# Sixteen Strassen blocks in the first matrix of a fused attention and two-matrix kernel, with copied C11 starts and accumulating DMAs

## The chip, the core and the metric

The kernel runs on one core of one Trainium2 chip. Its time is what the device takes for one execution, in microseconds (us). TensorE (PE) multiplies matrices and writes PSUM (8 banks of 128 x 512 f32); VectorE (DVE) and ScalarE (ACT) read PSUM and work on SBUF; GpSimd (POOL) and SyncE (SP) mostly issue DMAs here. Each engine runs its own instructions in order.

## What is computed

Attention with 4 batches, 8 heads, 768 positions and 64 channels, over the last 96 positions and 8 global ones, with a linear bias by distance. Its output, 3072 tokens of 512, goes through two matrices:

```python
scores = scale * q @ k^T + bias          # kept where local (0 <= i-j < 96) or global (j < 8)
x = softmax(scores) @ v                  # 3072 x 512
h = x @ w_in                             # 512 -> 2048
g = h - tanh(h)
out = g @ w_out                          # 2048 -> 512
```

## The kernel before

The 3072 tokens are 24 units of 128 queries. A unit u goes through words (steps) whose order on all five engines is one long string, ORDER, read from left to right and issued as it stands; a second string, HOMES, gives each tile's buffer or PSUM bank. A word is a step, a unit or group, and a part; "/a", "/d", "/p" or "/s" after it puts it on ACT, DVE, POOL or SP. The words that matter here:

- lq, lk, lv: loads of q, k and v by POOL (line 342); T.u: q and k transposed, by TensorE for the first seven units and from u = 7 by SP's DMA transposes (L377); V.u, K.u: copies of the 8 global rows.
- S.u: scores (PE, L396); E.u: exponential (ACT, L403); M.u: mask (DVE); AV.u: P·V (PE, L427); R, N: division by the sums (DVE, L433, L444); X or Xe: x transposed, by PE or by SP's DMA (L466).
- First matrix: units form groups of 1, 2 or 4. Plainly, m1.g.f are the matmuls of one block (L477), th.g.f the tanh (ACT, L576), g.g.f the subtraction to g (DVE, L590).
- A Strassen block (g, j) of the first matrix, four units by four slices of 128 columns: seven products d1 to d7 (in_product, L536) of 4 matmuls 128 x 256, in place of 8 halves; e0, e1, e2 copy partial results out of PSUM, q11, q21, q22 add (L547, L550), and tanh and subtraction take two slices at once (L562, L568). x and w_in sums (y and v) feed them.
- Second matrix, in pairs of units, all Strassen: n1 to n4 sum g (L630), p1 to p7 are the products (L645, 8 matmuls 128 x 256), a0 to a2 copy partial results (line 274 on ACT, 276 on DVE), c11 to c22 form results (L659), st stores (L662). w1 to w4 are the sums of w_out.

POOL's queue holds all loads and half the stores in order; SP's queue the DMA transposes and the other stores. A DMA on either that must wait (for a buffer, a landed load) holds all that is behind it.

Of the kernel before, what the change touches and what calls it, by code (L numbers as in the profile page):

```python
# [7 lines left out]
FP32 = mybir.dt.float32  # L8
BF16 = mybir.dt.bfloat16
# [8 lines left out]
lq.1 lk.1 zero rel ones.0 zero:7 dist lq.2 lq.0 lk.0 zero:7 zero:7 table lq.3 turn zero:7 first zero:7 lk.3 ident slopes  # L18
zero:7 zero:7 lk.2 ones.1 B.0 lv.1 cq.1/a ck.1/d bm.1 lv.0 T.1.1 em.1 lv.2 T.1.0 Te.1.1/d B.1 cq.0/a lv.3 Te.1.0/d
ck.0/a T.0.0 S.1 in.0 Te.0.0/a T.3.0 B.2 E.1.0 in.1 Te.3.0/d T.0.1 Te.0.1/d in.3 T.2.1 T.3.1 Te.2.1/a T.2.0 Te.3.1/d S.0  # L20
lq.4 Te.2.0/a AV.1 E.0.0 S.2 R.1 N.1/d in.2 B.3 E.2.0 lk.4 AV.0 S.3 R.0 N.0/d X.1 in.4 E.3.0 AV.2 Xe.1/d X.0 in.5 R.2
N.2/d bm.2 Xe.0/a AV.3 m1.1.0 lk.5 em.2 R.3 N.3/d X.2 m1.0.0 th.1.0 Xe.2/d X.3 lq.5 th.0.0 g.1.0 m1.0.2 Xe.3/a g.0.0
m1.1.2 th.0.2 m1.2.2 th.1.2 g.0.2 g.1.2 lv.4 m1.2.6 th.2.2 lk.6 g.2.2 T.4.0 th.2.6 m1.2.0 Te.4.0/a m1.1.4 lq.6 th.2.0
m1.0.4 lv.5 th.1.4 g.1.4 T.4.1 m1.2.4 Te.4.1/a g.2.0 th.0.4 S.4 th.2.4 g.0.4 out.1 m1.1.8 K.4/a E.4.0 g.2.6 m1.2.8
th.1.8 M.4.0 E.4.1 m1.0.8 g.1.8 th.2.8 out.0 M.4.1 m1.0.12 th.0.8 g.2.4 out.2 T.5.1 g.2.8 T.5.0 Te.5.1/a m1.1.12 out.3
Te.5.0/d th.0.12 g.0.8 S.5 lk.7 th.1.12 g.0.12 AV.4 E.5.0 g.1.12 lq.7 m1.2.12 n1.0/d E.5.1 lk.10 m1.2.10 M.5.0 lq.10
V.4/a R.4 m1.2.14 M.5.1 th.2.10 K.5/d N.4/d AV.5 th.2.14 T.6.1 X.4 R.5 Te.6.1/a T.6.0 N.5/d lq.9 Xe.4/a Te.6.0/d X.5 S.6
Xe.5/d g.2.14 m1.3.2 E.6.1 n3.0/d m1.3.10 g.2.10 lq.8 th.2.12 w1.1 th.3.2 p1.0 E.6.0 w1.0 m1.3.12 g.2.12 a0.0/a g.3.2
m1.3.4 lk.8 th.3.12 n2.0/d K.6/a th.3.10 m1.3.0 w2.0 m1.3.8 w4.0 w2.1 lk.9 p2.0 M.6.0 p6.0 lv.7 g.3.12 w3.1 T.7 m1.3.6
lv.6 a1.0/a c11.0 th.3.0 w3.0 p5.0 g.3.10 p7.0 a2.0/a n1.2/d th.3.4 g.3.0 p1.2 th.3.6 n2.2/d p2.2 a0.2/a w4.1 th.3.8  # L30
c22.0 p6.2 V.5/a n4.2/d T.8 p4.0 n3.2/d a1.2/a g.3.8 T.9 p5.2 g.3.6 p7.2 c21.0 a2.2/a T.10 g.3.4 st.1.0/p p3.2 M.6.1
lk.11 c11.2 S.7 c12.2/a c22.2 lv.11 n4.0/d AV.6 E.7.1 p4.2 lk.12 R.6 N.6/d E.7.0 m1.3.14 lv.9 K.7/d V.6/d M.7.1 X.6
lk.16 th.3.14 p3.0 M.7.0 Xe.6/a c21.2 lq.11 AV.7 g.3.14 c12.0/a lk.13 R.7 S.8 N.7/d lq.12 n1.4/d X.7 E.8.1 p1.4 Xe.7/d
lv.10 n2.4/d m1.4.8 K.9/a E.8.0 v1.1 st.2.0/p n3.4/d m1.4.10 th.4.8 a0.4/d lv.8 g.4.8 p6.4 th.4.10 v2.1 E.9.0 lq.13
m1.4.14 g.4.10 M.8 a1.4/a S.9 th.4.14 T.11 p5.4 g.4.14 E.9.1 V.7/d p2.4 a2.4/d E.10.0 M.9 T.12 m1.4.2 E.10.1 n4.4/d
m1.4.6 K.10/a st.0.0/s M.10 AV.9 th.4.6 m1.4.0 th.4.2 g.4.6 m1.4.4 R.9 T.13 N.9/d p7.4 g.4.2 th.4.4 Xe.9 th.4.0 g.4.4
AV.8 V.9/a p3.4 c11.4 c22.4 R.8 m1.4.12 N.8/d c12.4/a st.4.0/p g.4.0 p4.4 Xe.8 th.4.12 lq.15 v3.1 S.10 c21.4 lk.15
g.4.12 p1.6 E.12.0 lv.13 n1.6/d p2.6 n2.6/d a0.6/a lq.14 E.11.1 K.12/d AV.10 lk.14 p6.6 E.11.0 R.10 c11.6 V.10/d lq.16
m1.5.10 N.10/d a1.6/a K.11/a n4.6/d lv.12 S.11 th.5.10 n3.6/d T.15 p5.6 g.5.10 E.12.1 v1.3 m1.5.8 E.13.1 M.12 m1.5.14
a2.6/a th.5.8 T.14 M.11 m1.5.12 E.13.0 m1.5.6 v3.3 th.5.12 Xe.10 v4.1 th.5.14 g.5.12 p3.6 th.5.6 g.5.8 T.16 AV.11 g.5.14  # L40
m1.5.2 g.5.6 m1.5.0 V.11/d th.5.2 R.11 N.11/d c12.6/a p7.6 th.5.0 st.6.0/p g.5.2 Xe.11 lk.17 AV.12 g.5.0 m1.5.4 c22.6
# [24 lines left out]
q22.9.2 d2.9.3 n2.18/d p1.18 q21.9.1 g.9.2 d4.9.2 a0.18/a d5.9.3 n4.16/d d7.9.3 e2.9.3/a q11.9.3 p7.16 th.9.6 q22.9.3
d3.9.3 c11.16 a2.16/a p6.18 n3.18/d q21.9.2 m1.9.3 g.9.6 p3.16 th.9.3 c22.16 a1.18/a d4.9.3 th.9.12 g.9.3 p5.18 q21.9.3
th.9.10 g.9.12 p4.16 a2.18/a p2.18 g.9.10 th.9.14 p7.18 c12.16/a n4.18/d st.16.0/p p1.20 c22.18 g.9.14 p3.18 a0.20/a
p4.18 n1.20/d n2.20/d p2.20 n3.20/d p6.20 n1.22/d c21.16 p7.20 n4.20/d a1.20/a st.17.0/p p5.20 n3.22/d c21.18 p2.22
c11.18 a2.20/a st.19.0/s n2.22/d c12.18/a p1.22 st.18.0/s c22.20 c11.20 p4.20 a0.22/a c11.22 p6.22 n4.22/d st.22.0/s  # L70
c21.20 p7.22 a1.22/a st.21.0/p p5.22 p3.20 a2.22/a c22.22 p3.22.0 c12.20/a p4.22 st.20.0/s c12.22.0/d st.22.256/s
p3.22.1 c21.22 c12.22.1/d st.23.0/s st.22.384/s
"""
HOMES = """
v.0:1 tr.0.1:6 tr.0.0:6 kq.0:2 qk.0:6 v.1:0 tr.1.1:6 tr.1.0:7 kq.1:0 qk.1:5 v.2:2 tr.2.1:7 tr.2.0:5 kq.2:1 qk.2:8 v.3:3
tr.3.1:4 tr.3.0:7 kq.3:3 qk.3:7 v.4:4 tr.4.1:3 tr.4.0:1 kq.4:4 qk.4:9 v.5:5 tr.5.1:4 tr.5.0:5 kq.5:0 qk.5:18 v.6:6
tr.6.1:7 tr.6.0:1 kq.6:1 qk.6:4 v.7:4 kq.7:0 qk.7:16 v.8:8 kq.8:1 qk.8:3 v.9:5 kq.9:17 qk.9:2 v.10:6 kq.10:19 qk.10:10
# [44 lines left out]
def kernel(  # L122
# [27 lines left out]
    WJ = 4  # L150
# [692 lines left out]
```

## Time and profile before

| | |
|---|---|
| time, median of 3 runs | 202.04 us (201.58 to 202.12) |
| span of the profiled execution, first to last instruction | 199.8 us |
| what lies between the two | 2.2 us |
| PE, DVE, ACT, POOL busy | 97%, 89%, 68%, 38% |
| matmuls | 2219 |
| clock granted to TensorE | 1.000 |
| moved by DMA | 27.36 MB |

The profiled execution's own time is given as its span; the median of the runs is the time that the kernel is measured by. Busy time adds overlapping matmuls and is not TensorE at its peak. In a row of a group the columns are busy time, mean ns of one, and idle time of the engine before it with what ended that; in a row of the chain or the timeline they are start, length and what ran.

### The profile page before, as it was taken

The numbers are of one execution on the slowest core, as the hardware profiler recorded it, in microseconds if no ns is written. First come the engines' busy times: TensorE is split into PE (matmuls) and PEld (weight loads), VectorE is DVE, ScalarE is ACT, GpSimd is POOL, SyncE is SP. The second block draws the span as 40 slices with busy tenths as digits, with TensorE's granted clock in tenths as the row PEclk, the third lists the DMA queues.
The fourth block names the chain that finished last, engine by engine and source line by source line (L and its number), as shares of the span: only waits on it lengthen the run. The fifth ranks groups of instructions, "written<-read, shape, count | busy, mean of one in ns | idle before, by whom it ended". The sixth has DMA issues, their size and how long they took to land.

```text
span 199.8 us, 5524 instructions
## 1 busy us (share of the span) xinstructions
PE 193.1 (97%) x2219; PEld 157.8 (79%) x2219; DVE 178.6 (89%) x348; ACT 135.1 (68%) x234; POOL 75.3 (38%) x97
## 2 busy tenths in 40 slices
PE   8799999999999999999999999999999999999992
PEld 2469998888888988988898655688898687888892
DVE  6487599999999999999999898999999999999942
ACT  3698898726569559758947789578778777464220
POOL 8987576350694057069207904702000100001110
PEclk9999999999999999999999999999999999999999
DMA  5999999999999999989996998994733101001233
GB/s 148 211 180 185 198 163 207 201 156 141 193 167 196 178 153 135 133 188 171 137 158 146 140 173 192 154 155 85 55 108 121 66 0 54 3 0 52 107 132 131
DMA packets 103545, 27.36 MB, mean 137 GB/s; under 512 B 93920, under 2 KB 101472, under 8 KB 103520
## 3 DMA queue, kind: packets, MB, share of 16 engines
q0 software_dynamic: 74048, 16.78, 89.5%
q1 hardware_dynamic: 28928, 9.70, 27.6%
q10 hardware_dynamic: 544, 0.52, 1.0%
q8 instruction: 17, 0.28, 0.5%
q14 instruction: 8, 0.07, 0.1%
HBM read 27.26 MB, written 6.29 MB: 168 GB/s over the span
## 4 chain that ended last, share of the span: by engine, by line
PE 85%; DVE 7%; DMA 3%; ACT 2%; issue 1%; ACTq 0%; DVEq 0%
PE ps L645 36%; PE ps L477 27%; PE ps L536 9%; PE ps L396 5%; PE ps L427 5%; DMA f<-in_q_dram 3%; DVE gall L590 2%; DVE x L444 2%; DVE mem L407 1%; PE ps L455 1%; ACT mem L403 1%; PE ps L320 1%; ACT mem L274 1%; PE ps L365 1%; ACT th L576 1%
## 5 line engine op out<-in xcount | busy, mean ns | idle before, releaser
L477 PE MATMUL ps<-xT,w_in_bf 128*128 128x256 bf16 (+2 forms) x544 | 69.0, 279 | 0.0
L477 PEld LDWEIGHTS <-w_in_bf 128*128 128x128 bf16 x544 | 47.2, 98 | 12.4
L576 ACT ACTIVATE th<-ps 128x512 f32<-128x512 f32 (+1 forms) x74 | 41.8, 591 | 18.7 <-PE ps L477 13.6
L590 DVE TENSOR_TENSOR gall<-ps,th 128x512 bf16<-128x512 f32 (+1 forms) x74 | 47.4, 668 | 6.0 <-ACT th L576 5.6
L645 PEld LDWEIGHTS <-gall 128*128 128x128 bf16 x488 | 46.4, 98 | 7.0
L662 POOL DMA_DIRECT2D out_dram<-ot x14 | 8.1, 580 | 102.5 <-ACT ot L274 52.4
L403 ACT ACTIVATE mem<-ps 128x1024 bf16<-128x1024 f32 x44 | 43.3, 1024 | 4.3 <-PE ps L396 4.2
L645 PE MATMUL ps<-w_out_bf,gall 128*128 128x256 bf16 (+1 forms) x296 | 36.3, 270 | 0.0
L274 ACT COPY sn<-ps 128x256 f32<-128x256 f32 x32 | 12.0, 375 | 20.3 <-PE ps L645 16.3
L645 PE MATMUL ps<-f,ss 128*128 128x256 bf16 x192 | 24.9, 273 | 0.0
L645 PE MATMUL ps<-wc,gall 128*128 128x256 bf16 x192 | 24.9, 273 | 0.0
L342 POOL DMA_DIRECT2D vb<-in_v_dram x24 | 21.5, 900 | 2.2 <-issue 1.0
L645 PEld LDWEIGHTS <-ss 128*128 128x128 bf16 x192 | 18.3, 98 | 2.8
L342 POOL DMA_DIRECT2D mem<-in_k_dram x20 | 17.9, 899 | 4.8 <-DMA w_out_bf<-in_moe_w_out_dram 3.1
L342 POOL DMA_DIRECT2D mem<-in_q_dram x20 | 18.1, 904 | 3.8 <-DMA w_out_bf<-in_moe_w_out_dram 3.0
L412 DVE TENSOR_TENSOR mem<-mem,mk 128x2048 bf16<-128x2048 bf16 x16 | 19.2, 1215 | 0.0
L659 DVE TENSOR_TENSOR ot<-ps,sn 128x256 f32<-128x256 f32 x36 | 14.7, 415 | 3.6 <-ACT sn L274 2.5
L444 DVE TENSOR_TENSOR x<-ps,rden 128x512 bf16<-128x512 f32 x23 | 15.8, 687 | 0.5
L274 ACT COPY mem<-ps 128x512 f32<-128x512 f32 (+1 forms) x22 | 12.7, 585 | 5.1 <-PE ps L536 3.9
L427 PEld LDWEIGHTS <-mem 128*128 128x128 bf16 x352 | 13.4, 97 | 2.1 <-ACT mem L403 0.5
L427 PE MATMUL ps<-vb,mem 128*128 128x65 bf16 x352 | 14.7, 193 | 0.0
L396 PE MATMUL ps<-mem 64*128 64x128 bf16 x352 | 13.1, 217 | 0.0
(78 smaller groups left out, 220.7 us busy)
## 6 DMA issues: line engine op xcount, KB each, us to landing
out_dram<-ot POOLq DMA_DIRECT2D x14, 256.0 KB, 2.8
vb<-in_v_dram POOLq DMA_DIRECT2D x24, 128.0 KB, 6.2
mem<-in_q_dram POOLq DMA_DIRECT2D x22, 128.0 KB, 6.3
mem<-in_k_dram POOLq DMA_DIRECT2D x22, 128.0 KB, 6.1
out_dram<-ot SPq DMA_DIRECT2D x9, 256.0 KB, 2.0
w_out_bf<-in_moe_w_out_dram POOLq DMA_DIRECT2D x4, 512.0 KB, 10.7
w_in_bf<-in_moe_w_in_dram POOLq DMA_DIRECT2D x4, 256.0 KB, 7.6
w_in_bf<-in_moe_w_in_dram POOLq DMA_DIRECT2D x2, 512.0 KB, 11.0
```

Of the source, the lines that this page charges most:

```text
L274: nc.scalar.copy(out=out, in_=in_)
L342: eng(e).dma_start(out=dst, in_=rows_of(src, u).rearrange("h p d -> p h d"))
L396: nc.tensor.matmul(bank(("s", u, o), hh)[:, p * P : (p + 1) * P], buf(("qk", back[u] if o else u))[r, 1, p, :], buf(("qk", u))[r, 0, p, :] ...
L403: nc.scalar.activation(d, banks(("s", u, o), 0, 1), AF.Exp, bias=0.0, scale=scale)
L412: nc.vector.tensor_tensor(out=t, in0=t, in1=mk[:, 1:3], op=ALU.mult)
L427: nc.tensor.matmul(t[:, h // (H // 2), h % (H // 2), :], buf(("p", u, o))[:, slot(h), :], buf(("v", back[u] if o else u))[:, h, 0 : Dh + 1 ...
L444: nc.vector.tensor_tensor(out=buf(("x", u)).rearrange("q (a h) d -> q a h d", a=2), in0=t[:, :, :, 0:Dh], in1=rden.to_broadcast([P, 2, H / ...
L477: nc.tensor.matmul(t[:, (f - f0) * n : (f - f0 + 1) * n], w_in_bf[j][:, c, fo : fo + P], x[:, c, 0:n], start=(c == 0), stop=(c == CD - 1),)
L536: nc.tensor.matmul(t[:, r * 2 * P : (r + 1) * 2 * P], w(r)[:, c], x[:, c], start=first and r + c == 0, stop=c == 1, skip_group_check=not f ...
L576: nc.scalar.activation(h_view(buf(("th", g, f0)), g, m), h_view(bank(("h", g, f0)), g, m), AF.Tanh, bias=0.0, scale=1.0)
L590: nc.vector.tensor_tensor(out=o, in0=v(h), in1=v(th), op=ALU.subtract)
L645: nc.tensor.matmul(bank((holder, a))[:, c0:c1], s(f), t(f)[:, c0:c1], start=first and f == 0, stop=f == HF - 1, skip_group_check=not first,)
```

## The change

Sixteen blocks (groups 5 to 8, all four j) of the first matrix are Strassen blocks, in place of six; units 8 to 11 form one group of four in place of two pairs. In both matrices the first product that starts C11 is copied by ACT from its PSUM bank to C11's bank (a0, e0), and the second product (p2, d2) adds to it there, so that C11 is a plain copy and the additions q11 go. In groups 6 to 8 the z sums are copied by ACT to memory (x21, x22) and added by accumulating DMAs from POOL (q21, q22); nine n3 and five n4 are accumulating DMAs too. Eight of the V copies are made by SP's DMA. The signs of the w_out sums, the layout of g and the columns of a Strassen product in its bank are others, and ORDER and HOMES are new throughout.

```diff
-    NM, NV, NG, NSS, NSN = 23, 12, 5, 5, 4
+    QUADS = 8
+    NM, NV, NG, NSS, NSN, NXT = 20, 12, 5, 3, 4, 3
-    DUNITS = [(8, 1), (8, 2), (8, 3), (9, 1), (9, 2), (9, 3)]
+    DUNITS = [(g, j) for g in range(5, 9) for j in range(4)]
+    ADDED = range(6, 9)
...
-    groups = [[u] for u in range(SINGLE)] + [[u, u + 1] for u in range(SINGLE, 12, 2)] + [[u, u+1, u+2, u+3] for u in range(12, NU, 4)]
+    groups = [[u] for u in range(SINGLE)] + [[u, u + 1] for u in range(SINGLE, QUADS, 2)] + [
+        [u, u + 1, u + 2, u + 3] for u in range(QUADS, NU, 4)]
...
     def a_V(e, u):
-        copy(e, buf(("v", u))[0:G, :, 0:Dh], buf(("v", head[u]))[0:G, :, 0:Dh])
+        o, i = (buf(("v", t))[0:G, :, 0:Dh] for t in (u, head[u]))
+        if e is SP:
+            nc.sync.dma_start(out=o, in_=i)
+        else:
+            copy(e, o, i)
...
     def in_product(g, j, k):
...
-            2: ("q", lambda r: w_in_of(a + r, 2), x_block(g, 2, 1), True),
+            2: ("q", lambda r: w_in_of(a + r, 2), x_block(g, 2, 1), False),
...
-        t = d_bank(g, j, part)
+        t = d_bank(g, j, part).rearrange("q (t r n) -> q t r n", t=2, r=2)
         for r in range(2):
             for c in range(2):
                 nc.tensor.matmul(
-                    t[:, r * 2 * P : (r + 1) * 2 * P], w(r)[:, c], x[:, c], start=first and r + c == 0, stop=c == 1,
+                    t[:, :, r, :], w(r)[:, c], x[:, c], start=first and r + c == 0, stop=c == 1,
...
     def d_add(g, j, k):
-        if k == 0:
-            q = d_bank(g, j, "q")
-            nc.vector.tensor_tensor(out=q, in0=q, in1=d_keep(g, j, 0), op=ALU.add)
-            return
         a = d_keep(g, j, k)
+        if g in ADDED:
+            nc.gpsimd.dma_start(out=a, in_=buf((f"z{k}", g, j)), accum_op=ALU.add)
+            return
         nc.vector.tensor_tensor(out=a, in0=d_bank(g, j, "z"), in1=a, op=ALU.add)
...
     def g_sum(e, a, k):
...
+        if e is POOL:
+            nc.gpsimd.dma_start(out=o, in_=y, accum_op=ALU.add)
+        else:
+            eng(e).tensor_tensor(out=o, in0=x, in1=y, op=ALU.add)
...
     def keep(e, a, k):
-        copy(e, buf(("sn", a, k)), bank(("r", a))[:, 0:DH2])
+        copy(e, buf(("sn", a, k)) if k else bank(("q", a))[:, 0:DH2], bank(("r", a))[:, 0:DH2])
...
     def result(e, a, i, j, c0=0, c1=DH2):
-        if (i, j) == (1, 2):
-            copy(e, o, bank(("r", a))[:, c0:c1])
+        if i == 1:
+            copy(e, o, bank(("qr"[j - 1], a))[:, c0:c1])
             return
-        holder, k = {(1, 1): ("q", 0), (2, 1): ("z", 1), (2, 2): ("z", 2)}[i, j]
-        nc.vector.tensor_tensor(out=o, in0=bank((holder, a))[:, 0:DH2], in1=buf(("sn", a, k)), op=ALU.add)
+        nc.vector.tensor_tensor(out=o, in0=bank(("z", a))[:, 0:DH2], in1=buf(("sn", a, j)), op=ALU.subtract)
...
+            if g in ADDED:
+                op((f"x2{k}", g, j), ACT, lambda e, g=g, j=j, k=k: copy(
+                    e, buf((f"z{k}", g, j)), d_bank(g, j, "z")))
...
 ORDER (two stretches)
-g.2.8 T.5.0 Te.5.1/a m1.1.12 out.3
-Te.5.0/d th.0.12 g.0.8 S.5 lk.7 th.1.12 g.0.12 AV.4 E.5.0 g.1.12 lq.7 m1.2.12 n1.0/d E.5.1 lk.10 m1.2.10 M.5.0 lq.10
+out.3 lk.9 lv.6 lq.8 T.5.0
+g.2.8 Te.5.1/a m1.1.12 th.0.12 lv.20 Te.5.0/d lk.7 lq.7 T.7 lk.8 g.0.8 v1.0 S.5 th.1.12 g.0.12 AV.4 E.5.0 g.1.12
...
 HOMES (the words of units 7 and 8)
-v.7:4 kq.7:0 qk.7:16 v.8:8 kq.8:1 qk.8:3
+kq.7:5 v.7:5 kq.8:10 v.8:4
+qk.7:12 qk.8:5
```

kq is where a unit's q and k are loaded, qk where their transposes go; the number is the buffer of mem.

How the order moves on POOL, behind the last load of w_out. vb6 and vb7 are the v of units 6 and 20, mem the q and k of a unit. Before, the first two rows of mem are k and q of unit 7 (lk.7, lq.7):

```order
31 L348 DMA w_out_bf3_79<-in_moe_w_out_dram 128x4x512
32 L342 DMA mem_81<-in_k_dram 128x8x64
33 L342 DMA mem_81<-in_q_dram 128x8x64
34 L342 DMA mem_81<-in_k_dram 128x8x64
35 L342 DMA mem_81<-in_q_dram 128x8x64 x3
36 L342 DMA mem_81<-in_k_dram 128x8x64 x2
37 L342 DMA vb4_86<-in_v_dram 128x8x64
38 L342 DMA vb6_88<-in_v_dram 128x8x64
39 L662 DMA out_0_dram<-ot1_114 128x512
```

Now they are lk.9, lv.6, lq.8, lv.20, then lk.7 and lq.7, lk.8 and lq.9, and the accumulating n3.0:

```order
31 L356 DMA w_out_bf3_79<-in_moe_w_out_dram 128x4x512
32 L350 DMA mem_81<-in_k_dram 128x8x64
33 L350 DMA vb6_88<-in_v_dram 128x8x64
34 L350 DMA mem_81<-in_q_dram 128x8x64
35 L350 DMA vb7_89<-in_v_dram 128x8x64
36 L350 DMA mem_81<-in_k_dram 128x8x64
37 L350 DMA mem_81<-in_q_dram 128x8x64
38 L350 DMA mem_81<-in_k_dram 128x8x64
39 L350 DMA mem_81<-in_q_dram 128x8x64
40 L651 DMA gall_102<-gall_102 128x1024
```

The loads of unit 7 have moved from the first and second place to the fifth and sixth.

On ACT, before, from the last exponentials (E.23, first row) on; mem<-ps of 512 are e1 and e2 and e0, sn is a0, vb the copies V.21 and V.22:

```order
118 L403 ACTIVATE mem<-ps 128x1024 x2
119 L274 COPY mem<-ps 128x512
120 L274 COPY sn_111<-ps 128x256
121 L274 COPY vb_88<-vb_85 8x8x64
122 L274 COPY mem<-ps 128x512
123 L576 ACTIVATE th<-ps 128x512
124 L274 COPY mem<-ps 128x512 x2
125 L562 ACTIVATE th<-ps 128x1024
126 L274 COPY mem<-ps 128x512
```

Now, with the exponentials of units 20 to 23 (L412) among tanh of two slices (L578), copies x21 and x22 to mem and the copies e0 from bank to bank (ps<-ps 512); the last row of them here is e0.7.0:

```order
134 L578 ACTIVATE th<-ps 128x1024
135 L412 ACTIVATE mem<-ps 128x1024 x3
136 L578 ACTIVATE th<-mem 128x1024
137 L412 ACTIVATE mem<-ps 128x1024 x3
138 L578 ACTIVATE th<-mem 128x1024
139 L282 COPY mem<-ps 128x512 x2
140 L412 ACTIVATE mem<-ps 128x1024
141 L282 COPY ps<-ps 128x512
142 L412 ACTIVATE mem<-ps 128x1024
143 L282 COPY mem<-ps 128x512 x2
144 L282 COPY ps<-ps 128x512
```

The Strassen steps of groups 6 and 7 now stand among the last units' exponentials, where before they came behind them.

More of the change, by code (lines that the diff above doesn't have):

```diff
@@ L68 @@
[L68 to L72, printed above, removed]
+lk.1 lq.1 zero zero:7 zero:7 zero:7 zero:7 zero:7 zero:7 zero:7 rel ones.0 lq.2 dist lk.0 lq.0 lq.3 turn table first
@@ L478, in m1 @@
                     t[:, (f - f0) * n : (f - f0 + 1) * n], w_in_bf[j][:, c, fo : fo + P], x[:, c, 0:n],
-                    start=(c == 0), stop=(c == CD - 1),
+                    start=f == f0 and c == 0, stop=(c == CD - 1),
+                    skip_group_check=f > f0,
                 )
@@ L494, in wsum @@
     def wsum(j, k):
-        return four(("ws", j))[:, k - 1]
+        return ws[:, j, k - 1]
     def xsum(g, k):
@@ L758 @@
         for k in range(3):
-            op((f"e{k}", g, j), None, lambda e, g=g, j=j, k=k: d_copy(e, g, j, k))
-        for w, k in (("q11", 0), ("q21", 1), ("q22", 2)):
-            op((w, g, j), DVE, lambda e, g=g, j=j, k=k: d_add(g, j, k))
+            op((f"e{k}", g, j), None if k else ACT, lambda e, g=g, j=j, k=k: d_copy(e, g, j, k))
+        for w, k in (("q21", 1), ("q22", 2)):
+            op((w, g, j), POOL if g in ADDED else DVE, lambda e, g=g, j=j, k=k: d_add(g, j, k))
+            if g in ADDED:
+                op((f"x2{k}", g, j), ACT, lambda e, g=g, j=j, k=k: copy(
+                    e, buf((f"z{k}", g, j)), d_bank(g, j, "z")))
     for x in range(2):
```

268 lines of the change are left out of this document (142 added, 126 removed).

## The prediction

> **What bounds the kernel now.** I read the page's busy times and slices first, then the chain that ended last, then the timelines of the queues around the places that the change moves.
>
> ```profile
> span 199.8 us, 5524 instructions
> PE 193.1 (97%) x2219; PEld 157.8 (79%) x2219; DVE 178.6 (89%) x348; ACT 135.1 (68%) x234; POOL 75.3 (38%) x97
> PE   8799999999999999999999999999999999999992
> DVE  6487599999999999999999898999999999999942
> PEclk9999999999999999999999999999999999999999
> DMA  5999999999999999989996998994733101001233
> PE 85%; DVE 7%; DMA 3%; ACT 2%; issue 1%; ACTq 0%; DVEq 0%
> ```
>
> TensorE is the bound: busy in every slice, at an even clock, and 85% of the chain. VectorE is close behind (89%), ScalarE has room on average, and the DMA engines are full for the first two thirds. So a matmul that is saved is worth its time only if neither VectorE, ScalarE nor a transfer becomes late in the same stretch. The chain gives the price of each kind of TensorE work, since its rows carry no overlap:
>
> ```profile
> 15.41 0.45 PE ps L477 x8
> 25.79 0.92 ACT mem L403
> 34.92 0.56 PE ps L396 x16
> 43.57 0.87 PE ps L477 x8
> 52.31 0.55 PE ps L396 x16
> 62.61 0.78 PE ps L396 x24
> 66.99 0.48 PE ps L427 x16
> 152.52 0.44 PE ps L536 x4
> 178.65 17.12 PE ps L645 x160
> 195.80 0.42 DVE ot L659
> ```
>
> A block of the first matrix (L477: 8 matmuls 256 wide, or as many columns in other widths) takes 0.87, a Strassen block's one product (L536) 0.44, one of the second matrix's (L645) 17.12/20 = 0.86, scores of one unit (L396) 0.55 or 0.78, P·V (L427) 0.48. I count from the end of S.4, the scores of unit 4, because everything ahead of it is the same work in nearly the same order (16.7 us of TensorE in both):
>
> ```profile
> 23.46 0.62 PE L396 MATMUL ps<-mem 64*128 64x128 bf16 x16
> 24.01 3.73 PE L477 MATMUL ps<-xT,w_in_bf 128*128 128x128 bf16 x56
> 56.71 0.84 PE L396 MATMUL ps<-mem 64*128 64x128 bf16 x24
> ```
>
> From 24.0 to the end of the last product at 195.8 are 171.8 us; the work in it, counted from the program at those prices, is 168.7. So TensorE waits 3.1 us in all: up to the end of S.8 (57.5, where 32.0 us of work make 56.0) 1.5, behind it 1.6. The remaining 4.0 are the last result, the last stores and the end. The profiled 199.8 stand 2.2 under the median of the runs, 202.04; I add every difference to the median.
>
> **TensorE work: -4.4.** Behind S.4 the scores, P·V, transposes and the second matrix's products are the same in number. The first matrix's 64 plain blocks become 24, and its Strassen products 42 become 112: 40 x 0.872 off, 70 x 0.436 on, 34.9 - 30.5 = 4.4 us less. That C11 starts from a copied bank changes no count: p2 and d2 only stop clearing their bank.
>
> **VectorE: -11 of work, nothing by itself.** Rows that price what goes and comes:
>
> ```profile
> L590 DVE TENSOR_TENSOR gall<-ps,th 128x512 bf16<-128x512 f32 x70 | 45.8, 682 | 5.5 <-ACT th L576 5.2
> L659 DVE TENSOR_TENSOR ot<-ps,sn 128x256 f32<-128x256 f32 x36 | 14.7, 415 | 3.6 <-ACT sn L274 2.5 <-PE ps L645 0.8
> L630 DVE TENSOR_TENSOR gall<-gall 128x1024 bf16<-128x1024 bf16 x12 | 8.2, 681 | 0.0
> L568 DVE TENSOR_TENSOR gall<-ps,th 128x1024 bf16<-128x1024 f32 x6 | 7.3, 1219 | 0.0
> L550 DVE TENSOR_TENSOR mem<-ps,mem 128x512 f32<-128x512 f32 x12 | 8.2, 682 | 0.0
> ```
>
> Off: 40 plain subtractions (27.3), 14 g sums (9.5), 12 result additions (5.0), 10 Strassen additions (6.8). On: 20 subtractions over two blocks (24.4), x and w_in sums (some 5) and some 15 copies out of PSUM that the new order gives to it (9). That is 11 less, but VectorE is not what TensorE waits for in most of the program, so it only gives slack. In one stretch it gets tighter: the w_in and w_out sums that stood behind 37 us now stand between M.4.0 and the first products, where VectorE is full already; by the same prices I find 1.8 us more of its work there than of TensorE's. That lies ahead of S.7 and inside the next term.
>
> **Transposes of units 7 and 8: +6.0, the largest term.** Here are the two queues as they ran, POOL with the loads and SP with the transposes of q and k. The three landing lines are those of the loads (L342) from 28 to 46 us, of the transposes (L377) from 38 to 54, and of all 17 transposes; the last two rows are the page's DMA issues:
>
> ```profile
> 27.45 0.74 POOL L348 DMA_DIRECT2D w_out_bf<-in_moe_w_out_dram  x1
> 28.62 0.89 POOL L342 DMA_DIRECT2D mem<-in_k_dram  x1 [0.43 <-PE ps L356]
> 29.50 0.88 POOL L342 DMA_DIRECT2D mem<-in_q_dram  x1
> POOL mem L342 <- DMA w_out_bf<-in_moe_w_out_dram: 6.0, 4, 1.9
> DMA to landing us min/median/max: 6.5/10.7/13.7
> 43.24 1.33 SPq L377 DMA_TRANSPOSE mem<-mem  x1
> 46.73 4.26 SPq L377 DMA_TRANSPOSE mem<-mem  x2
> DMA to landing us min/median/max: 5.0/5.8/8.3
> DMA to landing us min/median/max: 3.1/5.4/8.3
> vb<-in_v_dram POOLq DMA_DIRECT2D x24, 128.0 KB, 6.2
> out_dram<-ot POOLq DMA_DIRECT2D x14, 256.0 KB, 2.8
> ```
>
> The loads of unit 7 are the two rows at 28.62 and 29.50, right behind the last load of w_out. They queue behind it on full DMA engines: the longest landing of this window is 13.7 us, and 29.50 + 13.7 = 43.2 is when T.7 is issued. T.7 has the 8.3 (43.24 + 8.3 = 51.5), and S.7 starts at 52.31 without a wait: before, it was just in time. Now four loads (lk.9, lv.6, lq.8, lv.20) stand ahead of those two. Each is 0.88 of issue, and the queue passes them at about that pace, so lq.7 lands 4 x 0.88 = 3.5 later and T.7 is issued at 46.8. T.8, which was issued at 46.73 beside T.7, now writes where T.7 reads: its queue holds it until T.7 has landed. Behind it on SP wait T.10, V.7 and T.12.
>
> At the median of all, 5.4 for a transpose, T.7 lands at 52.2 and T.8 at 57.6. Between S.4 and S.7 stand 23.0 us of TensorE work (16 blocks of the first matrix, 6 products, 3 P·V, 2 scores, the small transposes), 4 us less than before, since six products moved behind it and a P·V and a block ahead of it; from S.7 to S.8 0.5 + 2.6. So without waits S.8 would start at 24.0 + 23.0 + 3.1 = 50.1, and it waits to 57.6: 7.5 us, the VectorE stretch within them. From this I take off the 1.5 that before loses up to there: **+6.0**. Bounds: with the fastest, 3.1, for both, 46.8 + 6.2 = 53.0, 2.9 of wait, +1.4; with 8.3 and 5.5, 60.6, 10.5 of wait, +9.0.
>
> The Trainium skill (Advanced Engine Details and Errata, "X-Bar Transpose (TRN2)") says that transpose DMAs on this chip are as fast as regular DMAs. Here they are not quicker than the loads, 5.4 against 6.2, but slower than a store of 256 KB, 2.8; at that price T.7 and T.8 would land at 46.8 + 5.6 = 52.4, 2.3 of wait, which would make the term +0.8 and the whole -1.4, rival A's side.
>
> **ScalarE: +2.2 in one stretch.** Prices:
>
> ```profile
> L403 ACT ACTIVATE mem<-ps 128x1024 bf16<-128x1024 f32 x44 | 43.3, 1024 | 4.3 <-PE ps L396 4.2
> L562 ACT ACTIVATE th<-mem 128x1024 f32<-128x1024 f32 x6 | 6.4, 1059 | 1.4 <-DVE mem L550 1.2 <-DVE gall L568 0.2
> L274 ACT COPY mem<-ps 128x512 f32<-128x512 f32 x18 | 10.3, 585 | 4.1 <-PE ps L536 3.9
> L274 ACT COPY sn<-ps 128x256 f32<-128x256 f32 x32 | 12.0, 375 | 20.3 <-PE ps L645 16.3 <-DVE ot L659 3.4 <-DVE mem L509 0.5
> ```
>
> Back to back each takes 0.10 less than its mean (scores' exponential 1.024 in the group, 0.92 in the chain). ScalarE gets about 23 us more to do: 40 tanh of 512 go, 20 of 1024 come, some 29 copies of 512 to memory, and 28 copies from bank to bank, which no row shows. Those I bound by the nearest rows of the same sizes, 0.585 and 0.375 (a copy that stays in PSUM could be a tenth quicker or slower), and take the rows. On average this fits: 172 of 200. It does not fit between e1.6.1 and e0.7.0: two copies at the ends, 8 exponentials, 7 tanh, 12 copies of 512 and one of 256 are 8 x 0.92 + 7 x 0.95 + 14 x 0.48 + 0.27 = 21.0 us, while TensorE has 18.8 us of work between d6.6.1, which frees the first, and d6.7.0, which needs the last: +2.2 at least, if ScalarE is never idle there. Taken 1.0 lower if the copies are quicker, 1.0 higher for one late accumulation.
>
> **Edits at nothing, with their cover.** The 38 accumulating DMAs are not in the trace; issue 0.58 as a store of 256 KB, landing between the store's 2.8 and a load's 6.2. I take 2.8, since most of the 24 for z fall behind 140 us, where the DMA slices empty, and then each lands before the tanh or product that wants it; at 6.2 they cost (rival B). They also queue on POOL in order, and n3.0 and q22.6.2 there hold the loads behind them. The eight V copies by SP cost VectorE and ScalarE nothing; two stand between T.7 and T.10. The end: c21.20 (0.42) and a store of 256 KB (2.0 on SP, 2.8 on POOL) against 0.42, 0.29 and a store of 64 KB (1.8): 0 to +0.8, taken 0. The 1.6 us of TensorE's waits behind S.8 stay.
>
> **Sum:** -4.4 + 6.0 + 2.2 = +3.8, so 199.8 + 3.8 = 203.6 for the span and 202.04 + 3.8 = **205.8** for the time. With the low ends, -4.4 + 1.4 + 1.2 = -1.8: 200.2; with the high ends, -4.4 + 9.0 + 3.2 + 0.8 = +8.6: 210.6.
>
> **Rivals.** *A, the transposes come in time.* If lq.7 lands where the load in its place landed before with less queued behind it, and transposes run at 3.1, S.7 and S.8 wait only for VectorE's stretch, which is about the 1.5 that before lost too: -4.4 + 0.3 + 2.2 = -1.9, 200.1, and 198.1 if ScalarE's stretch finds 2 us elsewhere. For it: POOL's next instruction behind the loads, n3.0, waits for VectorE, and then fewer loads crowd the transposes. Against: 5.0 was the least that any took in that window. It decides when T.8 lands before 57.6 - 3.8 = 53.8, where the sum is 0.
>
> *B, accumulating DMAs gate the tanh.* At a load's 6.2 each accumulation is 3.4 later. th.6.10 and th.6.14 stand in ScalarE's full stretch with about 1.5 of slack, and p3.4 waits for n4.4, which is issued behind some twenty loads: 2 x (3.4 - 1.5) + 1.5 = +5.3 on top, 211. For it: POOL is in order, the last loads stand between the accumulations of group 6, and the DMA slices up to 140 us are full. Against: from there they are at 4 to 7 tenths and below.
>
> *C, the strided output.* The Strassen products now write two runs of 128 per row of the bank instead of one of 256. The nearest row, blocks of the first matrix 128 wide, is hardly dearer per column (8 in 0.45 in the chain's row at 15.41, against half of 0.87), so it is 0 in the sum; twice the time for 448 matmuls would be 448 x 0.109 = +49, 255 us. The Trainium skill (PSUM — Partial Sum Buffer, "Specifications (TRN2)") says that any non-contiguous access pattern slows matmuls significantly, which speaks for C; no run here shows such a pattern.
>
> **How the numbers follow.** The forecast has 0.52, A 0.30, B 0.15, C 0.03. Medians of this kernel differ by some 0.3%, 0.6 us, so faster means below 201.4 and slower above 202.6. A is mostly below: 0.29 in all. Between lies the forecast's low edge, 0.07. Slower gets 0.64. The range takes A's middle and part of B: 199.5 to 210.5.
>
> **What would show it.** Right: S.7 and S.8 start late behind SP's transposes, TensorE idle 4 to 9 us between 45 and 60 us, put down to DMA mem; later a wait of about 2 us for ScalarE's copies or tanh around the stretch of units 20 to 23; L536 matmuls at the same price. Wrong: TensorE dense from 47 to 60 us (A), waits for POOL's DMAs ahead of L578 or behind n4.4 (B), L536 matmuls dearer (C), or a new wait that none of these names.

## The result, and the profile after

The changed kernel takes **296.07 us** (294.67 to 298.54, 3 runs) against 202.04, a ratio of 1.466 [1.4536, 1.4785]. Slower was the likelier side, but 205.8 with a range up to 210.5 missed by 90 us, so the right direction says little for the forecast. The lines of the page that answer to those of before:

```profile
span 292.8 us, 5747 instructions
PE 214.8 (73%) x2275; PEld 173.9 (59%) x2275; DVE 175.9 (60%) x319; ACT 158.2 (54%) x263; POOL 106.2 (36%) x131
PE   8899779645877179828977676676773869877793
DVE  6657899816636068764865157365572467648752
ACT  4977766735448138426754367654770467654410
PEclk9999999968979759986997689777998899999999
DMA  7999999999999963999124249996089556685243
PE 7%; DVE 2%; ACT 0%; issue 0%; DVEq 0%
```

No engine is full: TensorE falls from 97% to 73%, VectorE from 89% to 60%. The matmuls are as many as was counted, 2275: 224 of the plain blocks less and 280 of Strassen products more than 2219. From the fifth slice on (some 29 us) TensorE has gaps, and from the eighth (51 us) it is rarely full, as are the others: they wait for each other. The chain can be followed back only over the last 10% of the span. The granted clock (PEclk), which stood at 9 in every slice before, now dips. Where the waits end, six rows of the view of all waits (us in total, times, longest):

```profile
ACT mem L282 <- PE ps L550: 29.2, 18, 6.9
ACT mem L412 <- PE ps L404: 18.2, 8, 6.2
PE ps L668 <- ACT mem L412: 14.6, 8, 3.0
DVE x L457 <- DMA xT<-x: 10.9, 4, 6.0
PE ps L440 <- ACT mem L412: 5.8, 4, 3.1
PE ps L404 <- DMA mem<-mem: 2.1, 1, 2.1
```

The third row is the odd one. L668 are the second matrix's products and L412 the scores' exponentials: they share no data. The timeline shows one case, in which they share no bank either: S.8 (from there on one S takes the scores of a unit and a half, here unit 8 and half of unit 9), its three exponentials, and p7.0:

```profile
59.31 0.85 PE L404 MATMUL ps<-mem 64*128 64x128 bf16 x24 [2.13 <-DMA mem<-mem]
60.24 2.85 ACT L412 ACTIVATE mem<-ps 128x1024 bf16<-128x1024 f32 x3 [2.65 <-PE ps L404]
63.15 1.23 PE L668 MATMUL ps<-wc,gall 128*128 128x256 bf16 x5 [2.99 <-ACT mem L412]
```

The exponentials end at 60.24 + 2.85 = 63.09, and p7.0 starts 0.06 later after a wait of 2.99. By HOMES p7.0 writes bank 4 (z.0:4) and the last exponential, E.8.1, reads banks 1 and 5 (s.8.1:1,5). Bank 4 is touched by neither half; it lies between them. This is what the experiments went after first: an instruction on two banks is written as one access with a step, `ps[:, x : y + 1 : y - x, :]`, and every two-bank access of before has neighbours, (0,1) to (6,7), while most pairs of after lie apart: 73 of the 124 instructions of ScalarE and VectorE on two banks, against none of 105 before.

### The profile page after: what moved, and what is told of

The parts are those of the page before. It is cut to its first block, busy times and chain, and to the rows that moved or that the text cites. A ratio compares the mean times of both kernels' runs of the same rounds, so it can differ in the third digit from the quotient of the medians.

```text
span 292.8 us, 5747 instructions
## 1 busy us (share of the span) xinstructions
PE 214.8 (73%) x2275; PEld 173.9 (59%) x2275; DVE 175.9 (60%) x319; ACT 158.2 (54%) x263; POOL 106.2 (36%) x131
## 5 line engine op out<-in xcount | busy, mean ns | idle before, releaser
L668 PEld LDWEIGHTS <-gall 128*128 128x128 bf16 x488 | 50.0, 105 | 24.8 <-issue 13.9
L412 ACT ACTIVATE mem<-ps 128x1024 bf16<-128x1024 f32 x44 | 43.3, 1025 | 23.6 <-PE ps L404 18.2
L561 POOL DMA_DIRECT2D mem<-mem x24 | 21.3, 984 | 78.4 <-ACT mem L282 57.1
L282 ACT COPY mem<-ps 128x512 f32<-128x512 f32 (+1 forms) x51 | 29.2, 587 | 32.6 <-PE ps L550 29.2
L550 PE MATMUL ps<-mem,ws 128*128 128x256 bf16 x192 | 30.6, 292 | 21.4 <-ACT mem L282 8.1
L550 PEld LDWEIGHTS <-ws 128*128 128x128 bf16 x256 | 26.1, 103 | 29.2 <-issue 24.7
L668 PE MATMUL ps<-w_out_bf,gall 128*128 128x256 bf16 (+1 forms) x296 | 38.7, 281 | 5.2 <-ACT mem L412 3.4
L668 PE MATMUL ps<-wc,gall 128*128 128x256 bf16 x192 | 29.1, 308 | 9.0 <-ACT mem L412 3.6
L668 PE MATMUL ps<-f,ss 128*128 128x256 bf16 x192 | 27.9, 297 | 7.6 <-ACT mem L412 7.6
L490 PE MATMUL ps<-xT,w_in_bf 128*128 128x256 bf16 (+1 forms) x320 | 31.9, 253 | 1.2 <-DVE gall L608 1.0
L608 DVE TENSOR_TENSOR gall<-ps,th 128x512 bf16<-128x512 f32 (+1 forms) x34 | 21.8, 656 | 14.1 <-ACT th L593 9.0
L584 DVE TENSOR_TENSOR gall<-ps,th 128x1024 bf16<-128x1024 f32 x16 | 19.6, 1223 | 13.0 <-ACT th L578 7.1
L668 PEld LDWEIGHTS <-ss 128*128 128x128 bf16 x192 | 20.1, 105 | 11.6 <-issue 7.7
L593 ACT ACTIVATE th<-ps 128x512 f32<-128x512 f32 (+1 forms) x34 | 18.9, 578 | 10.5 <-PE ps L490 7.5
L578 ACT ACTIVATE th<-ps 128x1024 f32<-128x1024 f32 x16 | 16.4, 1025 | 12.9 <-DVE mem L563 5.0
```

The lines of the kernel that those rows point to most:

```text
L282: nc.scalar.copy(out=out, in_=in_)
L412: nc.scalar.activation(d, banks(("s", u, o), 0, 1), AF.Exp, bias=0.0, scale=scale)
L490: nc.tensor.matmul(t[:, (f - f0) * n : (f - f0 + 1) * n], w_in_bf[j][:, c, fo : fo + P], x[:, c, 0:n], start=f == f0 and c == 0, stop=(c = ...
L550: nc.tensor.matmul(t[:, :, r, :], w(r)[:, c], x[:, c], start=first and r + c == 0, stop=c == 1, skip_group_check=not first or r > 0,)
L561: nc.gpsimd.dma_start(out=a, in_=buf((f"z{k}", g, j)), accum_op=ALU.add)
L578: nc.scalar.activation(d_tanh(g, f), h_of(g, f), AF.Tanh, bias=0.0, scale=1.0)
```

## The experiments

Medians are in us. The kernel before measured 202.04, 201.54, 201.5, 201.78 and 201.71 in the groups of runs; ratios are to it.

**The kernel before with its banks renumbered.** One permutation of bank numbers in HOMES, by which the neighbours (0,1) become 0 and 4, and so on; order, work and data are the same:

```diff
- s.8.0:6,7  s.8.1:2,3  av.8:4,5 ...
+ s.8.0:3,7  s.8.1:1,5  av.8:2,6 ...   # 0,1,2,3,4,5,6,7 -> 0,4,1,5,2,6,3,7 throughout
```

> The kernel before with its eight PSUM banks renumbered (0 1 2 3 4 5 6 7 become 0 4 1 5 2 6 3 7) and nothing else: same order, same work, same buffers. Every access to two banks at once, which was to neighbours, now goes to banks four apart. Theory R (an access to two banks that lie apart is made to wait, and be waited for, as if it covered every bank between them): much slower, 260 us or more, with TensorE waits of 1 to 4 us ended by exponentials and subtractions of other banks. Theory A (the 94 us come from the accumulating DMAs and the queues behind them): 202.0, no change within 0.3%.

Measured: **276.55**, 1.3688 [1.3642, 1.3734]. Names of banks alone cost 74 us. From its page and its waits:

```profile
span 275.2 us, 5524 instructions
PE   8648977689678795698888688877786689399994
PEclk9965899999979999999999999968599799979999
ACT mem L403 <- PE ps L645: 15.9, 12, 2.9
PE ps L477 <- ACT mem L403: 13.1, 12, 2.2
PE ps L427 <- ACT mem L403: 7.2, 9, 1.8
```

Exponentials (L403) now wait for second-matrix products, and the first matrix's blocks (L477) for exponentials, in both directions. No such row stands among the waits of before, where an exponential waits for little but its own scores:

```profile
ACT mem L403 <- PE ps L396: 4.2, 7, 1.1
```

**The same, with each access to two banks cut in two.** An exponential, a division or a Strassen block's tanh and subtraction is issued once for each bank when the two lie apart:

```diff
+    def cuts(x, y):
+        return [slice(0, 2)] if abs(y - x) == 1 else [slice(0, 1), slice(1, 2)]
-        nc.scalar.activation(d, banks(("s", u, o), 0, 1), AF.Exp, bias=0.0, scale=scale)
+        for i in cuts(*home(("s", u, o))):
+            nc.scalar.activation(d[:, i], banks(("s", u, o), 0, 1)[:, i], AF.Exp, bias=0.0, scale=scale)
```

> The kernel before with its banks renumbered, as in the first experiment, and now every ACT or DVE instruction on two banks (all of them are apart) cut into two. Theory R: the 74 us of the renumbering go again and only the added instructions stay, some 44 exponentials at 0.06, 24 divisions at 0.06 and 24 reciprocals at 0.1 us: 203 to 208 us. Against R: it stays above 240.

Measured: **203.14**, 1.0063 [1.0041, 1.0086]. The renumbered banks stay and the 74 us are gone:

```profile
span 202.1 us, 5640 instructions
PE   8798999999999999999999999999999999999992
PEclk9999999999999999999999999999999999999998
ACT mem L407 <- PE ps L399: 3.9, 7, 1.0
```

So neither the banks nor their distance are slow; the single access over them is what other engines wait for. What is left, 0.6%, goes with 103 more instructions on ScalarE and VectorE.

**The changed kernel with the same cuts.** 28 of 44 pairs of exponentials, 11 of the divisions' and 12 of 16 Strassen blocks' were cut.

> The changed kernel in which each ACT or DVE instruction that reads two banks that are not neighbours is cut into two, one for each bank (exponentials, reciprocals and divisions of 24 units, tanh and subtraction of the Strassen blocks); the same order and buffers, some 70 more instructions. Theory R: the waits on other banks go and the time falls to 200 to 215 us. Theory A: it stays at 290 or rises by the added instructions.

Measured: **255.25**, 1.2607 [1.2554, 1.2661], 41 us less. Theory R had the direction and not the size: some 53 us above before remain. The place shown above now reads:

```profile
62.68 1.46 PE L407 MATMUL ps<-mem 64*128 64x128 bf16 x24 [3.38 <-DMA mem<-mem]
63.30 2.98 ACT L416 ACTIVATE mem<-ps 128x512 bf16<-128x512 f32 x5 [3.60 <-PE ps L407]
64.07 1.89 PE L680 MATMUL ps<-wc,gall 128*128 128x256 bf16 x8
```

p7.0 starts while the exponentials run. But S.8 is late in this kernel too, by the transpose. Its chain can be followed from end to end, and a third of it is DMA:

```profile
PE 41%; DMA 33%; issue 8%; DVE 8%; ACT 6%; POOL 2%; SPq 1%; DVEq 0%; POOLq 0%; ACTq 0%
45.90 7.99 DMA mem<-mem
53.97 8.57 DMA mem<-mem
89.27 9.78 DMA xT<-x
99.86 7.14 DMA xT<-x
114.65 7.03 DMA xT<-x
```

**Accumulating DMAs as VectorE additions**, on the changed kernel and on the one with cuts:

```diff
-            op((w, g, j), POOL if g in ADDED else DVE, lambda e, g=g, j=j, k=k: d_add(g, j, k))
+            op((w, g, j), DVE, lambda e, g=g, j=j, k=k: d_add(g, j, k))
 ORDER: n3 and n4 of the 14 accumulating g sums
- n3.0 ... n4.4 ...
+ n3.0/d ... n4.4/d ...
```

> The changed kernel with its 38 accumulating DMAs replaced by VectorE additions at the same places of the order (24 x 0.99 and 14 x 0.68 us more VectorE work). Theory R: stays above 275. Theory A: falls to below 230.

> Both edits: two-bank accesses cut and accumulating DMAs replaced by VectorE additions. Under theory R the difference to the cut kernel alone is the net price of the accumulating DMAs: if their landings gate the tanh, faster than it by 3 us or more; if they are hidden, slower by up to the 30 us of added VectorE work, which I put at 5 to 15.

Measured: **282.88**, 1.4002 [1.3956, 1.4047], 13 us less than the changed kernel, and with the cuts **248.16**, 1.2283 [1.2243, 1.2323], 7 less than the cuts alone. The accumulating DMAs have a price, but they are not the main cause.

**Single reliefs of the kernel with cuts.** Five short ones. A third buffer for x, in turn over all units:

```diff
- x.8:0 x.9:1 x.10:0 x.11:0 x.12:0 ...
+ x.8:0 x.9:1 x.10:2 x.11:0 x.12:1 ...
```

> The cut kernel, with the x of units 8 to 23 in three buffers by turns, where mostly two were used (the third exists already). Theory Q (what is left of the 53 us is the chain through SP's queue: loads, transposes of q and k, transposes of x, which holds the divisions because both x buffers wait for a transpose): faster than 255 by 5 to 15 us. Theory D (the DMA engines are simply full, and each transpose takes what it takes): less than 3 us.

Measured: 254.16, 1.2599 [1.2506, 1.2693]; a miss. Unit 7's loads first, and buffers by which T.8 need not wait for T.7:

```diff
- out.3 lk.9 lv.6 lq.8 ... lv.20 Te.5.0/d lk.7 lq.7 T.7      kq.7:5  qk.8:5
+ out.3 lk.7 lq.7 lk.9 lv.6 lq.8 ... lv.20 Te.5.0/d T.7      kq.7:13 qk.8:18
```

> The cut kernel, with the loads of unit 7 again first behind those of w_out, into a buffer of their own, and the transposes of unit 8 in another, so that T.8 waits for no buffer of T.7. My prediction's term: T.7 is issued near 43 and T.8 near 47 us, S.8 starts at 53 to 56 instead of 62.7, and the time falls by 4 to 8 us. Theory Q agrees; theory D: S.8 earlier, but the time by less than 2, since the later transposes set it.

Measured: 260.72, 1.2924 [1.283, 1.3018], 5 us worse. T.7 took 9.9 us from issue to landing (42.6 to 52.5) instead of 8.0. T.8 waited for no buffer any more, but it was issued at 51.3 and not near 47 (54.0 in the kernel with cuts), right behind T.9 and V.6, which stand ahead of it on SP, and took 9.6 to land; S.8 started at 60.9 instead of 62.7. Why the whole was slower is not shown. The eight copies of V by VectorE instead of SP's DMA (`V.6/s` to `V.6/d`, and so on):

> The cut kernel, with the eight V copies on VectorE (0.36 us each) in place of SP's DMA. Theory Q: SP's queue no longer waits for P.V in front of T.8, T.10 and T.12, faster by 2 to 6 us. Theory D: within 2.

Measured: 256.26, 1.2703 [1.2552, 1.2854], nothing. The loads of far units (lv.20, lq.18, lk.22, lk.16, lq.22, lv.19, lk.21) moved back, and then also five stores from SP to POOL, ahead of its next loads:

```diff
- th.0.12 lv.20 ... lv.7 lq.18 ... a0.4 lk.22 ...
+ th.0.12 ... lv.7 ... a0.4 ... lv.18 lv.20 ... c22.6 lq.18 ... lv.21 lq.22 lk.22
- lq.11 st.0.0/s ... lk.14 st.2.0/s      (second kernel only)
+ lq.11 st.0.0/p ... lk.14 st.2.0/p
```

> The cut kernel with seven loads of far units (v of 20 and 19, k and q of 18, 16, 21 and 22, which the new order issues up to 60 us before their use) moved behind the loads of nearer units. Theory G (loads of far units crowd the near transposes: 8 to 14 us for a transpose of q and k, where before it took 5): T.8, T.14 and T.15 land 3 to 8 us earlier and the time falls by 4 to 15 us. Theory D (the sum of the transfers sets it, whatever their order) or Q: within 3 us.

> The same, and the first five stores (units 0, 1, 2, 4 and 5) on POOL's queue, as before, where each holds the loads behind it until its result is there, in place of SP's. Theory G: such a store keeps loads off the transposes; another 2 to 10 us faster, with shorter transposes between 70 and 100 us. Otherwise: slower, since the loads behind come later.

Measured: 256.42, 1.2725 [1.2551, 1.2899], and 254.2, 1.2614 [1.2547, 1.2682]. In the second S.12, the scores of units 14 and 15, started 6.6 us earlier (91.2 against 97.8), of which 2.3 were left at S.14 (138.7 against 140.9).

**Shorter loads.** q and k of units 7 to 23 loaded as contiguous rows of 2 KB, with the cuts, as a control on the kernel before, and with the DVE additions; the order of the elements is left out:

```diff
-  lambda e, u=u, j=j, src=src: load_natural(e, buf(("kq", u))[:, j, :]..., src, u)
+  lambda e, u=u, j=j, src=src: eng(e).dma_start(out=buf(("kq", u))[:, j, :],
+      in_=src[...].rearrange("h s d -> (h s) d")[...].rearrange("(p r) d -> p (r d)", r=8))
```

> The cut kernel, with the q and k of units 7 to 23 loaded as the same number of contiguous bytes (2 KB in a row per partition in place of eight pieces of 256 B); it leaves out the order of the elements, so the numbers that follow are others, the work the same. Theory D (the cut kernel's other 50 us are waits for loads and transposes: the new order wants them some 17 us of TensorE work earlier, while the DMA engines were full already before): the transposes come early and the time falls to 215 to 232 us. Theory Q (the order of the instructions in SP's and POOL's queues holds them, whatever the DMA engines do): above 245.

> The same short loads in the kernel before, as a control (the order of the elements is left out there too). Before, TensorE waited for no load, so under both theories 199.5 to 202: at most the 1 to 2 us of waits near units 5 to 8.

> The cut kernel with VectorE additions in place of the accumulating DMAs, and the short loads (the order of the elements is left out). Theory D: what the DMA engines still held is gone, 205 to 225 us, with VectorE or ScalarE as what TensorE waits for. If the accumulating DMAs only compete with the loads, it is no faster than with them; if their landings gate, faster by 5 or more.

Measured: 257.84 (254.14 to 261.55, too wide for a verdict), 202.47 at 1.0028 [1.0008, 1.0048], and 251.4 at 1.2462 [1.2408, 1.2517]. POOL issued such a load in 0.5 to 0.6 us instead of 0.9, and with the DVE additions the transposes landed about as fast as in before (medians 4.5 us for q and k, 3.7 for x, against 5.4 and 3.4). Yet nothing was gained: 251.4 is 3 us more than 248.16. So theory D fell, by which the sum of the DMA engines' work sets the time, and somewhat shorter transposes of q and k (5.8 in the kernel it is compared with) do not lower it by themselves.

**All of these reliefs together** (cuts, DVE additions, V on VectorE, three x buffers, unit 7 first, far loads later, stores on POOL):

> All edits at once: two-bank accesses cut, VectorE additions for the accumulating DMAs, V copies on VectorE, x in three buffers, unit 7 loaded first, far loads later, stores as gates. If what is left is only queues and transfers, 215 to 235 us. If it stays above 240, the order itself (scores and P.V pulled ahead of the products) lacks other work for TensorE.

Measured: **242.58**, 1.2038 [1.1977, 1.2099]. Still 41 us above before.

**No DMA transposes.** The rest was either waits for transposed tiles or the order of the engines' own work. So the transposes of q and k of units 7 to 23 were left out, then those of x too, on the kernel with cuts and DVE additions; then both on the kernel with all reliefs and on the kernel before:

```diff
     def a_DT(u):
-        nc.sync.dma_start_transpose(out=buf(("qk", u))..., in_=buf(("kq", u))...)
+        pass
     def buf(holder):
+        if k == "qk" and holder[1] >= PE_T:
+            return mk[:, 0].rearrange("q (a p) f -> q a p f", a=2)
+        if k == "xT" and groups[holder[1]][0] >= PE_X:      # not in the first
+            return w_in_bf[-1]
```

> The cut kernel with DVE adds (e4_cut_no_accumulate, 248.16), without the 17 DMA transposes of q and k of units 7 to 23 (the scores of these units read the mask's tile in their place, the key copies go to a tile of their own; the output is not the reference's); x is still transposed by DMA. Theory T (the order asks for transposed tiles earlier than DMA transposes can follow their loads, and this is the rest): 208 to 228, since S.8, S.12 and S.14 no longer wait and Xe meets emptier DMA engines. Theory O (the rest is the order of the work on TensorE, ScalarE and VectorE itself): 240 to 250.

> As e15, and the 16 DMA transposes of x are left out too (products of the first matrix for units 8 to 23 read a tile of w_in instead). Theory T: 202 to 212, TensorE's work plus ScalarE's and POOL's short waits. Theory O: 235 to 250.

> The kernel with all relief (e14_all_relief, 242.58), without both kinds of DMA transposes. Theory T: 200 to 210. Theory O: 230 to 243.

> Control: the kernel before without both kinds of DMA transposes. TensorE is dense there, so both theories expect 198 to 202.5; its 3 us of waits are all that can go.

Measured: **229.63**, 1.1365 [1.1293, 1.1437]; **224.43**, 1.1081 [1.0995, 1.1168]; 230.51, 1.1398 [1.1282, 1.1514]; and the control 200.57, 0.9964 [0.9923, 1.0006]. For the first two neither theory had it; the third lies at the low end of theory O. Waits for transposed tiles are 24 of the 46 us that stood open, 18.5 for q and k and 5.2 for x, and 22.7 remain without any. Such a kernel waits for the loads of q and k as little as for their transposes, and its first matrix no longer waits for x, so the runs price the tiles' lateness as a whole. On the kernel with all reliefs the same edit won 12.1 only. For the remainder, the page's busy times without transposes, then engines by stretch (start and end; length; busy us of PE, PEld, DVE, ACT, POOL; granted clock, DMA share, GB/s):

```profile
PE 195.2 (88%) x2274; PEld 163.6 (73%) x2275; DVE 193.9 (87%) x389; ACT 158.2 (71%) x303; POOL 72.6 (33%) x93
24.00:50.00 26.00, 24.20 (x319) 21.12 (x314) 25.46 (x52) 20.28 (x46) 15.85 (x20) 1.00 1.94 175
75.00:100.00 25.00, 23.63 (x305) 20.72 (x304) 23.31 (x45) 20.61 (x39) 11.97 (x14) 1.00 1.08 96
150.00:175.00 25.00, 21.98 (x231) 19.08 (x230) 23.62 (x42) 18.30 (x36) 0.00 (x0) 1.00 0.06 23
L570 DVE TENSOR_TENSOR mem<-mem 128x512 f32<-128x512 f32 x24 | 15.6, 681 | 0.0
```

VectorE is fuller than TensorE in the first and the last of these stretches and as full in the second, and about half of the chain between 158 and 205 us, 24 of 47, is VectorE's. It carries the 38 additions in place of the accumulating DMAs, some 26 us (24 at 0.681 in the last row above, 14 of the same length), which in this kernel no longer have a late tile to hide behind. That they are most of the 22.7 is argued, not shown: the kernel with cuts, accumulating DMAs and no transposes was not run.

## Why the prediction was wrong, by its own steps

The parts add up as follows, each measured on top of the one before: 296.07 for the change; 40.8 less when the pairs of banks are cut; 7.1 less with VectorE additions; 18.5 less without transposes of q and k; 5.2 less without those of x; 22.7 left. The sizes depend on this order: the cuts win 34.7 where the DVE additions are in already (282.88 to 248.16), and the additions 13.2 without the cuts.

**The step that failed is the count of the edits, which ends in "Edits at nothing, with their cover".** An edit that is not priced should stand there with a reason. HOMES was read for two words, the buffers of units 7 and 8; the new pairs of banks stand nowhere in the prediction, and so went into the sum at nothing without a reason. They are the largest single part, 40.8 of 94 us, and none of the rivals names them; the last sentence only left room for "a new wait that none of these names". Listing the pairs of HOMES on both sides would have shown the edit, though not its price.

**TensorE work, -4.4.** Its prices held: in the chain of the kernel with cuts a Strassen product of 4 matmuls takes 0.44, the 0.44 of before, so rival C, the strided output, is out. What the prediction quotes for it is not seen for this pattern. The row:

```profile
147.41 0.44 PE ps L556 x4
```

The gain of work is real, but a matmul that is saved is worth nothing on an engine that is idle for a quarter of the span.

**Transposes of units 7 and 8, +6.0.** Near in size at S.8, by another mechanism in part:

```profile
46.09 4.00 SPq L385 DMA_TRANSPOSE mem<-mem  x2
50.18 0.90 SPq L429 DMA_DIRECT2D vb<-vb  x1
51.20 5.56 SPq L385 DMA_TRANSPOSE mem<-mem  x2
DMA to landing us min/median/max: 8.0/8.0/8.0
```

T.7 was issued at 46.1 (predicted 46.8) and T.8 landed at 51.2 + 8.0 = 59.2 (predicted 57.6). S.8 started at 59.31, 9.2 after the 50.1 without waits; less the 1.5 of before that is +7.7. But T.8 left right behind V.6 on SP (50.18 + 0.90), ahead of the 52.2 at which T.7 was to let it go, and the excess is in its landing, 8.0 in place of 5.4. In the kernel with cuts it did wait for T.7, to 53.97. And only 2.1 us of TensorE's waits up to S.8 are put down to the transpose; other waits had made it late before, 2.2 us of them for exponentials.

The larger mistake is that the term ended there. I counted every unit up to 8 and took the waits behind it as unchanged, 1.6. The order also brings the scores of later units forward: without waits S.12 stands at 70.1 by the same count of TensorE work, against 87.1 before, 17 us sooner, while the loads and transposes it needs come no sooner. T.14, the last of them, was issued at 81.2 before and at 84.0 in the kernel with cuts; S.12 followed it by 8.3 us there and by 13.8 here. TensorE's delay in the kernel with cuts grows from 12.6 us at S.8 to 27.7 at S.12 and 38.5 at S.14. Without the q and k transposes (229.63 against 248.16) S.8 starts 8.8 us sooner, S.12 14.3 and S.14 18.6: the whole gain is there by S.14. That single reliefs gave nothing because the next tile was late too fits this, but was not shown tile by tile.

Transposes also got slower, above all those of x. The rows of all transposes, of before, of the kernel with cuts, and of that kernel with the DVE additions:

```profile
mem<-mem SPq DMA_TRANSPOSE x17, 5.4
xT<-x SPq DMA_TRANSPOSE x16, 3.4
```

```profile
mem<-mem SPq DMA_TRANSPOSE x17, 7.1
xT<-x SPq DMA_TRANSPOSE x16, 7.3
```

```profile
mem<-mem SPq DMA_TRANSPOSE x17, 5.8
xT<-x SPq DMA_TRANSPOSE x16, 3.5
```

Where the 38 accumulating DMAs are gone, with the same loads, most of the slowing is gone too, so it goes with them and not with the loads. For one transpose the bounds 3.1 to 8.3 nearly held (7.99 and 8.57 in the chain of the kernel with cuts); for two in a row 8.3 and 5.5 were too low. The sentence of the Trainium skill (Advanced Engine Details and Errata, "X-Bar Transpose (TRN2)") that they are as fast as regular DMAs is not settled by these rows. The prediction reads 5.4 as "not quicker" than the loads' 6.2, and it is quicker; than the stores' 2.8 it is slower.

**VectorE, -11 of work, nothing by itself.** The work is right, though its items add up to 10.2 and not 11: the kernel without transposes has 193.9 busy, less some 26 of added additions 168, against 178.6 before. The changed kernel itself has 175.9, since some instructions take longer in it (its 24 reciprocals 293 ns, 199 before). "Nothing by itself" held while VectorE had that slack; with the 38 additions given back to it, it may be what the rest waits for.

**ScalarE, +2.2.** The work is right to a tenth: "about 23 us more" against 158.2 - 135.1 = 23.1 (the "172 of 200" behind it should then be 158). The copies from bank to bank, which no row of before showed and which were bounded by the nearest rows, took 577 and 361 ns against the 585 and 375 taken:

```profile
L282 ACT COPY ps<-ps 128x512 f32<-128x512 f32 x16 | 9.2, 577 | 2.9 <-DVE gall L584 1.2 <-PE ps L550 0.9 <-DVE rden L446 0.7
L282 ACT COPY ps<-ps 128x256 f32<-128x256 f32 x12 | 4.3, 361 | 6.9 <-DVE rden L446 3.5 <-PE ps L668 1.6 <-DVE gall L584 1.3
```

Whether the stretch between e1.6.1 and e0.7.0 costs 2.2 can't be read: it lies behind larger delays in every kernel here.

**Accumulating DMAs, at nothing (rival B).** They landed after 5.3, 4.2 and 6.0 us, not 2.8, and issuing one takes POOL about 1.0 us, not 0.58:

```profile
mem<-mem POOLq DMA_DIRECT2D x24, 256.0 KB, 5.3
gall<-gall POOLq DMA_DIRECT2D x9, 256.0 KB, 4.2
gall<-ss POOLq DMA_DIRECT2D x5, 256.0 KB, 6.0
L561 POOL DMA_DIRECT2D mem<-mem x24 | 21.3, 984 | 78.4 <-ACT mem L282 57.1
```

Net of the VectorE time that they save they cost 7 to 13 us. Rival B's price, 5.3, was below both, and the nothing of the sum was not covered: a landing of 2.8 was taken from a plain store.

**What stays open.** The last 22.7 us (VectorE additions against other work of the order), and how the accumulating DMAs lengthen the transposes of x from 3.5 to 7.3 us. All reliefs with no transposes (230.51) are 6 us slower than no reliefs with none (224.43), and which relief costs that is not shown.

## What to carry to other kernels

Where one instruction reads or writes two places of a shared tile with a step, look at what lies between them: other engines may be made to wait for the whole stretch, and a table of buffer numbers then moves the time by a third without one instruction more. Price such a table as an edit of its own, by listing the pairs before and after. And when an order pulls matmuls forward, follow each of them to the last DMA that feeds it, not only the first two that move: if the loads and transposes stay where they were, the matmuls just wait there.

## What the runs showed of the hardware that was not expected

The waits on banks between two others are not the banks' own: the same banks with one instruction each cost 0.6% (203.14). The matmul above starts 0.06 us behind the exponential's end, and the profile puts its wait down to a semaphore of ScalarE. That speaks for a wait which the built program holds; the program itself was not read.

Waits have a second price, TensorE's clock. Before it was granted in full throughout; after it dips to 5 to 8 tenths in fifteen of its forty slices, and matmuls right behind a long wait take up to twice as long: S.8's 24 matmuls took 1.46 us behind a wait of 3.38 in the kernel with cuts, against 0.85 in the changed kernel behind 2.13, and the product behind it 1.89 where such a row has 1.04 elsewhere. That fits the Trainium skill (TensorE: Matmul & The Clock Gate, "Part 1: The HAM clock gate"), by which the clock falls to half after an idle window of some 3.4 us. Here the window was not wholly idle: in the changed kernel TensorE worked 0.85 us between 58.0 and 61.4, at a granted clock of 1.00, and from there to 68.2 the clock was 0.50. Some 156 matmuls at half pace make about 16 us of the changed kernel, an estimate from 0.21 against 0.109 each; they are inside the parts above, not beside them. That the clock follows the waits is shown by the renumbered kernel: the same work in the same order, dips in nine of its slices, and after the cut none but the 8 of the last slice.
